# Linear attention, an MLP and routed experts in one kernel: where the last blocks' router products run, and where the first expert tile's weights lie

## The chip, the cores and the metric

The kernel runs on one core of a Trainium2 chip. Its time is the device time of one execution in microseconds, a median of several runs. One more execution was profiled; all rows below come from it, with times in microseconds from its first instruction.

## The reference

Three stages, each feeding the next, on 2304 tokens (batch 4, 576 positions), in float32:

```
phi(x)  = [exp(p - m), exp(m - p)]   with p = x @ w_phi, m = max |p|          # 8 heads, 64 -> 2 x 128
attn    = (phi(q) @ (phi(k)^T v)) / (phi(q) . sum phi(k) + 1e-6)              # per head
y       = leaky_relu_0.01(attn @ w_in) @ w_out                                # 512 -> 2048 -> 512
logits  = (y / |y|) @ (emb / |emb|)^T / tau                                   # 8 experts
e, gate = argmax(logits), softmax(logits)[e]                                  # per token
out     = gate * (relu(y @ w1[e]) @ w2[e])                                    # 512 -> 1024 -> 512
```

## The kernel before, in words

Tokens are worked on in nine blocks of 256 (two tiles of 128) through attention and MLP. Products that need precision beyond one pass are split into a high and a low part, and three matmuls add up hi*hi, hi*lo and lo*hi. The MLP's inner width of 2048 is cut in sixteen chunks; a first loop over the blocks does chunks 0 to 7 and stores the half sums yp, a second loop does chunks 8 to 15. In it `mm1` makes h of a chunk, ScalarE and VectorE make t, g and gg of it (GpSimd the low half of gg), and `mm2` adds gg times the second weights into y. `y_half_b` ends a block: VectorE adds y and yp to ys (L606), SyncE stores ys, ScalarE squares it (L609), and then the logits are made, for blocks 0 to 7 by sixteen multiply-and-sum instructions on VectorE (L615; two tiles by eight experts, here called products, which read the embeddings `enb`), for block 8 on TensorE (L626, L634: eight transposes of ys and products with `ent`). `route` ranks the tokens of a block within their expert.

After block 5 a list of five tiles of 128 tokens is made for the most frequent expert (the early list), and a second list for the rest (late list, `make_list`, `list_ids`, `list_tail`) after block 8. The expert stage then walks over up to 25 tiles: `gather` fetches the tokens, `xT` transposes them, `up` and `down` are the two matmul stages, each in two halves of inner columns, `hT` transposes between. A tile's weights are four arrays of 128x2048 read to `raw`, and `split` (L921, L922) copies each to whi on ScalarE and subtracts to wlo on VectorE. These pairs lie in the buffers of the ring that held the MLP's second chunks, two buffers for a pair: pairs 1 to 3 use those of chunks 8 to 13. Pair 0 lies in a pool of its own, `ring_c`, that is opened in the space of `enb` and the products' scratch once these are closed, before block 8.

Each engine takes its instructions in order. The order is made when the program is built, by a scheduler with priorities; on TensorE the expert tiles' order is written out by hand, and on ScalarE that of tiles 0 and 1. Step (i, n) is a place in that written order: tile i, quarter n. `steps` names what of block 8 is put there: `ends` (its last two chunks of mm2, and the sums) at (0,1), then the four pieces `TAILS`, and the late list.

Of the kernel before, what the change touches and what calls it, by code (L numbers as in the profile page):

```python
# [9 lines left out]
F32 = mybir.dt.float32  # L10
F32R = mybir.dt.float32r
# [10 lines left out]
P = 128  # L22
B, H, S, D, F = 4, 8, 576, 64, 128
NTOK = B * S
DM = H * D
NPAIR = H // 2
DFF = 2048
NE = 8
EF = 1024
BLK = 256  # L30
NBLK = NTOK // BLK
NT = NTOK // P
NCH = 8
T_EARLY = 12
N_EARLY = 5
N_TILES = 25
N_PLAIN = 23
BIG = 8192.0
PRIO = 1000
J_PE = 8  # L40
J_UP = 9
W_DVE = tuple(range(16, 32))
N_HEAD = 3
# [16 lines left out]
GPOS2 = (5, 2)  # L60
MAN = (mybir.EngineType.PE,)
ENDS = (0, 1)
TAILS = ((1, 1), (1, 2), (2, 0), (2, 1))


@with_exitstack
def tile_attention_moe_router_experts(ctx, tc, qT, kT, va, w_phi, moew, emb, embT, tau, ew, out):
    nc = tc.nc
# [11 lines left out]
    def bc(ap, shape):  # L80
        return ap.to_broadcast(shape)


    ident = const.tile([P, P], F32, name="ident")
# [15 lines left out]
    for i in range(2):  # L100
        for r in range(2):
            nc.vector.tensor_copy(
                out=wblk[r * D:(r + 1) * D, i, r * F:(r + 1) * F],
                in_=wstk[r * D:(r + 1) * D, i, :].bitcast(F32),
# [3 lines left out]
    xg = ctx.enter_context(tc.tile_pool(name="xg", bufs=2, side="right"))  # L108
# [100 lines left out]
    qraw, qps, xr, xb = {}, {}, {}, {}  # L209
# [127 lines left out]
    yps = {}  # L337
# [20 lines left out]
    def mm2(j, c):  # L358
        c0 = c % NCH
        if c0 == 0:  # L360
            yps[j] = [ps_m.tile([P, DM], F32, tag="y", name="y") for _ in range(2)]
        gg, w = gs.pop((j, c)), wc[c]
        for t in range(2):
            ts = slice(t * P, (t + 1) * P)
            for a, b in ((0, 0), (0, 1), (1, 0)):
                nc.tensor.matmul(  # L366
                    yps[j][t], gg[:, a, ts], w[:, b, DM:2 * DM],
                    start=(c0 == 0 and a == 0 and b == 0), stop=(c0 == NCH - 1 and a == 1),
                )
# [80 lines left out]
    for j in range(NBLK):  # L450
# [15 lines left out]
        if j == NBLK - 1:  # L466
# [3 lines left out]
            ring_b = ctx.enter_context(tc.tile_pool(name="ring_b", bufs=8, side="left", reuse_waits="tile"))  # L470
# [35 lines left out]
    rt = ctx.enter_context(tc.tile_pool(name="rt", bufs=1, side="right", reuse_waits="tile"))  # L506
    ps_r = ctx.enter_context(tc.tile_pool(name="ps_r", bufs=1, space=PSUM))
    ps_t = ctx.enter_context(tc.tile_pool(name="ps_t", bufs=2, space=PSUM))
# [3 lines left out]
    def b_load(j):  # L512
        t = xg.tile([P, 2, 4, BLK], F32R, tag="xb", name="xb2")
        nc.gpsimd.dma_start(out=t, in_=xs_d[j])
        xb[j] = t
        y = xg.tile([P, 2, DM], F32, tag="yt", name="yt2")
        nc.sync.dma_start(out=y, in_=yp_d[j])
        ypt[j] = y

    b_load(0)  # L520
    lg_cm = tc.tile_pool(name="lg", bufs=1, side="right", reuse_waits="tile")
    lgp = lg_cm.__enter__()

    enb = lgp.tile([P, NE, DM], F32, name="enb")
    sst = rt.tile([P, NT], F32, name="sst")
    lg = rt.tile([P, NT, NE], F32, name="lg")
# [9 lines left out]
        out=upper, in_=upper, pattern=[[1, P]], compare_op=ALU.is_gt, fill=0.0, base=0, channel_multiplier=-1  # L536
# [45 lines left out]
    ent = rt.tile([P, 4, NE], F32, name="ent")  # L582
# [13 lines left out]

    def y_half_b(j):
        yt = ypt.pop(j)
        on_pe = j >= J_PE
        yss = []  # L600
        if not on_pe:
            lgr = rt.tile([P, 2, NE], F32, tag="lgr", name="lgr")
        for t in range(2):
            i = 2 * j + t
            ys = xg.tile([P, DM], F32, tag="ys", name="ys")
            nc.vector.tensor_add(ys, yps[j][t], yt[:, t, :])  # L606
            nc.sync.dma_start(out=y_d[i * P:(i + 1) * P, :], in_=ys)
            jk = xg.tile([P, DM], F32, tag="jk", name="jk", bufs=1)
            nc.scalar.activation(out=jk, in_=ys, func=AF.Square, accum_out=sst[:, i:i + 1])  # L609
            yss.append(ys)  # L610
            if on_pe:
                continue
            for e in range(NE):
                jk2 = lgp.tile([P, DM], F32, tag="jk2", name="jk2")
                nc.vector.tensor_tensor_reduce(  # L615
                    out=jk2, in0=ys, in1=enb[:, e, :], scale=1.0, scalar=0.0,
                    op0=ALU.mult, op1=ALU.add, accum_out=lgr[:, t, e:e + 1],
                )
        yps.pop(j)
        yield  # L620
        if on_pe:
            yTs = []
            for ys in yss:
                ps = ps_t.tile([P, DM], F32, tag="t", name="ytp")
                for k in range(4):
                    nc.tensor.transpose(ps[:, k * P:(k + 1) * P], ys[:, k * P:(k + 1) * P], ident)  # L626
                yT = xg.tile([P, DM], F32, tag="gg", name="yT", bufs=3)
                nc.scalar.copy(out=yT, in_=ps)
                yTs.append(yT)
            yield  # L630
            pl = ps_r.tile([P, 2, NE], F32, tag="pr", name="plg")
            for t in range(2):
                for k in range(4):
                    nc.tensor.matmul(  # L634
                        pl[:, t], yTs[t][:, k * P:(k + 1) * P], ent[:, k],
                        start=(t == 0 and k == 0), stop=(t == 1 and k == 3),
                    )
            lgr = pl
        nc.vector.tensor_tensor(
            out=lg[:, 2 * j:2 * j + 2, :], in0=lgr, in1=bc(esc.unsqueeze(1), [P, 2, NE]), op=ALU.mult  # L640
        )
        yield from route(j)
# [226 lines left out]
    def gather(i):  # L869
        xgt = m1.tile([P, DM], F32, tag="xgt", name="xgt")  # L870
        nc.gpsimd.indirect_dma_start(
            out=xgt, out_offset=None, in_=y_d[0:T_EARLY * P, :] if i < N_EARLY else y_d,
            in_offset=bass.IndirectOffsetOnAxis(ap=lists[i][1], axis=0),
        )
        xgs[i] = xgt
# [23 lines left out]
    def load_w(i, c):  # L899
        if i == 0 or i >= N_PLAIN:  # L900
            load_rows(i, c)
            return
        if i not in need:
            need[i] = nc.values_load(
                lists[i][2], engines=[mybir.EngineType.Pool], min_val=0, max_val=4 * NE
            )
        with tc.If(need[i] < NE):
            load_rows(i, c)
# [5 lines left out]
    pairs = {}  # L914
    changes = {}

    def split(c):
        hi, lo = pairs[c]
        for h in range(2):
            hs_ = slice(h * 1024, (h + 1) * 1024)  # L920
            nc.scalar.copy(out=hi[:, hs_], in_=raw[c][:, hs_])  # L921
            nc.vector.tensor_sub(lo[:, hs_], raw[c][:, hs_], hi[:, hs_].bitcast(F32))  # L922

    def first_split(c):
        pool = ring_c if c == 0 else ring_b
        pairs[c] = tuple(pool.tile([P, 2048], F32R, tag="W", name=n) for n in ("whi", "wlo"))
        split(c)
        load_w(1, c)

    def next_split(i, c):  # L930
# [6 lines left out]
        if i + 1 < N_PLAIN:  # L937
            load_w(i + 1, c)

    for j in range(NBLK):  # L940
        if j + 1 < NBLK:
            b_load(j + 1)
        last = j == NBLK - 1
        if last:
            lg_cm.__exit__(None, None, None)
            ring_c = ctx.enter_context(tc.tile_pool(name="ring_c", bufs=2, side="right", reuse_waits="tile"))
        with tc.high_priority(offset=2 * PRIO if j >= J_UP else 0):
            for c in range(NCH):
                mm1(j, NCH + c, 200 if j == 0 else 0)
                if c >= 2:  # L950
                    mm2(j, NCH + c - 2)
        if last:
            break
        mm2(j, 2 * NCH - 2)
        mm2(j, 2 * NCH - 1)
        for n, _ in enumerate(y_half_b(j)):
            pass
        xb.pop(j)
        if 2 * j + 2 == T_EARLY:
            with tc.high_priority(offset=PRIO):  # L960
                early_list = list_ids(*make_list(T_EARLY, N_EARLY, True))
                for c in range(4):
                    load_w(0, c)
                gather(0)
            xT(0)
            for _ in list_tail(*early_list):
                pass
# [91 lines left out]

    j = NBLK - 1  # L1060
    late = []
    tail = y_half_b(j)

    def ends():
        mm2(j, 2 * NCH - 2)
        mm2(j, 2 * NCH - 1)
        xb.pop(j)
        next(tail)

    steps = {  # L1070
        ENDS: ends,
        TAILS[0]: lambda: next(tail),
        TAILS[1]: lambda: next(tail),
        TAILS[2]: lambda: next(tail, None),
        TAILS[3]: lambda: late.append(make_list(NT, N_TILES - N_EARLY, False)),
        POS: lambda: late.append(list_ids(*late.pop())),
    }

    def hooks(i, n):
        if (i, n) in steps:  # L1080
            with tc.high_priority(offset=PRIO):
                steps[i, n]()
        if (i, n) == GPOS:
            late.append(list_tail(*late.pop(), after=acts[-K_ACT]))
            next(late[0])
        if (i, n) == GPOS2:
            next(late[0], None)

    for c in range(4):
        first_split(c)  # L1090
    with tc.manual_schedule(engines=set(MAN)):
        run(0, N_PLAIN, next_split, hooks)
# [60 lines left out]
```

## Time and profile before

| | |
|---|---|
| median of 3 runs | 927.18 us (926.13 to 929.4) |
| profiled execution | 925.01 us |
| its span, first to last instruction | 923.3 us |
| TensorE matmuls (PE) busy | 881.8 us, 96% |
| VectorE (DVE) busy | 553.2 us, 60% |
| ScalarE (ACT) busy | 450.2 us, 49% |
| GpSimd (POOL) busy | 225.3 us, 24% |
| mean granted clock of TensorE | 0.984 of full speed |

How to read it: a busy share is an average over stages, so it says which engine to look at, not where. Matmuls overlap in the records, so one lasts longer than its distance to the next. In the rows, PE is TensorE, DVE VectorE, ACT ScalarE, POOL GpSimd; the brackets at a row's end give the idle time of the engine before it and what ended it. The granted clock is a share of 2.4 GHz: 1.00 is full, 0.50 is 1.2 GHz.

### The profile page before, as it was taken

What the parts mean: (1) busy time and instruction counts of PE and PEld (TensorE: products, weight loads), DVE (VectorE), ACT (ScalarE), POOL (GpSimd) and SP (SyncE); (2) the same over time, 40 slices, a digit from 0 to 9 for tenths busy, and PEclk for the clock granted to TensorE, in tenths of its full rate; (3) what the DMA queues carried; (4) which work ended last, traced back from release to release, by engine and by line L of the source; (5) the groups of instructions that cost most, each with busy time, mean ns of one, the idle gap of its engine ahead of it and who ended that gap; (6) DMA issues with size and microseconds to landing.
All of it is one profiled execution on the core that took longest, in us unless ns stands there. A gap on an engine that the chain in (4) does not pass through costs nothing. (4 is left out here: it accounts for less than half of the span.)

```text
span 923.3 us, 18721 instructions
## 1 busy us (share of the span) xinstructions
PE 881.8 (96%) x7104; PEld 757.1 (82%) x7104; DVE 553.2 (60%) x1276; ACT 450.2 (49%) x904; POOL 225.3 (24%) x219
## 2 busy tenths in 40 slices
PE   8979999999999999899999999959999999999994
PEld 6768888889898888788888888838888888888883
DVE  6775557484765554748888899863422761113572
ACT  6965556484745654743333332523423862224571
POOL 2430113031111330033233333501113431113321
PEclk9989999999999999999999999979999999999998
DMA  8873423142130211943222221601014941114570
GB/s 280 290 239 99 133 75 127 50 123 103 48 107 24 104 69 61 324 166 112 86 103 92 98 89 65 240 23 36 28 49 149 351 150 47 41 41 168 183 265 31
DMA packets 42613, 112.36 MB, mean 122 GB/s; under 512 B 4558, under 2 KB 23118, under 8 KB 36496
## 3 DMA queue, kind: packets, MB, share of 16 engines
q1 hardware_dynamic: 33424, 61.48, 20.1%
q0 software_dynamic: 9008, 49.55, 15.4%
q8 instruction: 57, 0.93, 0.4%
q14 instruction: 44, 0.36, 0.1%
q10 hardware_dynamic: 80, 0.03, 0.0%
HBM read 87.45 MB, written 24.90 MB: 122 GB/s over the span
## 5 line engine op out<-in xcount | busy, mean ns | idle before, releaser
L366 PE MATMUL y<-W,gg 128*128 128x512 f32 x864 | 230.0, 400 | 1.0 <-ACT gg L353 1.0
L366 PEld LDWEIGHTS y<-W,gg 128*128 128x128 f32 x864 | 153.0, 189 | 29.0 <-ACT gg L353 1.4
L344 PE MATMUL h<-xb,W 128*128 128x256 f32 x576 | 164.3, 288 | 5.2 <-DVE g L351 3.3
L345 PE MATMUL h<-xb,W 128*128 128x256 f32 x576 | 162.7, 283 | 1.9 <-DVE xb L294 1.6
L346 PE MATMUL h<-xb,W 128*128 128x256 f32 x576 | 162.1, 283 | 0.0
L344 PEld LDWEIGHTS h<-xb,W 128*128 128x128 f32 x576 | 108.1, 189 | 13.3 <-DVE g L351 4.7
L345 PEld LDWEIGHTS h<-xb,W 128*128 128x128 f32 x576 | 108.5, 188 | 7.7 <-DVE xb L294 2.2
L252 POOL PARTITION_ALL_REDUCE qmx<-pr x28 | 56.4, 2016 | 221.6 <-ACT pr L234 218.0
L346 PEld LDWEIGHTS h<-xb,W 128*128 128x128 f32 x576 | 108.5, 189 | 1.6 <-issue 0.2
L353 ACT CAST gg<-g 128x256 fp32r<-128x256 f32 x144 | 57.5, 406 | 96.2 <-DVE g L351 87.5
L615 DVE CUSTOM_DVE_ANT_0 jk<-ys,enb 128x512 f32<-128x512 f32 x128 | 102.5, 801 | 2.0
L349 ACT ACTIVATE t<-h 128x256 f32<-128x256 f32 x144 | 54.5, 382 | 88.4 <-PE h L346 87.7
L351 DVE TENSOR_TENSOR g<-h,t 128x256 f32<-128x256 f32 x144 | 60.1, 420 | 53.4 <-ACT t L349 50.2
L355 POOL TENSOR_TENSOR gg<-g,gg 128x256 fp32r<-128x256 f32 x72 | 59.0, 823 | 134.5 <-ACT gg L353 117.7
L922 DVE TENSOR_TENSOR wlo<-raw,whi 128x1024 fp32r<-128x1024 f32 x56 | 68.1, 1255 | 36.0 <-ACT whi L921 30.3
L996 DVE TENSOR_TENSOR h<-htp,h 128x512 fp32r<-128x512 f32 x46 | 31.7, 689 | 92.9 <-ACTq L935 74.4
L978 PE MATMUL hps<-whi,xt 128*128 128x512 f32 x184 | 77.3, 420 | 9.9 <-ACT whi L921 9.8
L1008 PE MATMUL yo<-whi,h 128*128 128x512 f32 x184 | 74.7, 406 | 0.0
L979 PE MATMUL hps<-wlo,xt 128*128 128x512 f32 x184 | 73.7, 400 | 0.5 <-DVE wlo L922 0.5
L1009 PE MATMUL yo<-wlo,h 128*128 128x512 f32 x184 | 72.6, 395 | 0.0
L921 ACT CAST whi<-raw 128x1024 fp32r<-128x1024 f32 x56 | 55.9, 1047 | 34.2 <-PE hps L982 13.0
L985 ACT ACTIVATE hs<-hps 128x512 f32<-128x512 f32 x46 | 27.4, 595 | 71.3 <-PE hps L982 64.8
(239 smaller groups left out, 1600.0 us busy)
## 6 DMA issues: line engine op xcount, KB each, us to landing
wst<-in_moew_dram SPq DMA_DIRECT2D x32, 512.0 KB, 5.3
qraw<-in_q_dram SPq DMA_DIRECT2D x36, 256.0 KB, 3.0
xs_d<-xb SPq DMA_DIRECT2D x9, 1024.0 KB, 5.4
xb<-xs_d POOLq DMA_DIRECT2D x9, 1024.0 KB, 5.2
kraw<-in_k_dram SPq DMA_DIRECT2D x16, 288.0 KB, 3.3
yp_d<-yt SPq DMA_DIRECT2D x9, 512.0 KB, 3.7
yt<-yp_d SPq DMA_DIRECT2D x9, 512.0 KB, 3.8
y_d<-ys SPq DMA_DIRECT2D x18, 256.0 KB, 2.1
```

The source lines that it names most:

```text
L344: nc.tensor.matmul(hp, w[:, 0, ks], x[:, 0, k, :], start=(k == 0), stop=False)
L345: nc.tensor.matmul(hp, w[:, 0, ks], x[:, 1, k, :], start=False, stop=False)
L346: marks["mm1"] = nc.tensor.matmul(hp, w[:, 1, ks], x[:, 0, k, :], start=False, stop=(k == 3))
L351: nc.vector.tensor_tensor(out=g, in0=hp, in1=t, op=ALU.max)
L355: eng.tensor_sub(gg[:, 1, :], g, gg[:, 0, :].bitcast(F32))
L366: nc.tensor.matmul(yps[j][t], gg[:, a, ts], w[:, b, DM:2 * DM], start=(c0 == 0 and a == 0 and b == 0), stop=(c0 == NCH - 1 and a == 1),)
L615: nc.vector.tensor_tensor_reduce(out=jk2, in0=ys, in1=enb[:, e, :], scale=1.0, scalar=0.0, op0=ALU.mult, op1=ALU.add, accum_out=lgr[:, t, ...
L922: nc.vector.tensor_sub(lo[:, hs_], raw[c][:, hs_], hi[:, hs_].bitcast(F32))
L978: nc.tensor.matmul(ps, x[:, 0, k], hi[:, ks], start=(k == 0), stop=False)
L979: nc.tensor.matmul(ps, x[:, 0, k], lo[:, ks], start=False, stop=False)
L1008: nc.tensor.matmul(yacc[i], h2[:, 0, k], hi[:, w0], start=(nh == 0 and k == 0), stop=False)
L1009: nc.tensor.matmul(yacc[i], h2[:, 0, k], lo[:, w0], start=False, stop=False)
```

## The change

The logits of block 8 are made by products on VectorE, as for the other blocks; the TensorE variant goes (L626, L634). `enb` stays to the end, and `ring_c` with it goes: pairs 0 to 2 take the buffers of chunks 8 to 13, and pair 3, split inside `ends`, those of chunks 14 and 15. `y_half_b` stops once more, between the sums and the products, so that the products of blocks 7 and 8 can be put into steps (0,2) and (1,0), without the raised priority. The ranks of block 7 go to (1,3) and (2,1), those of block 8 to (2,2) and (3,0), the late list's making to (3,0).

```diff
-J_PE = 8
-TAILS = ((1, 1), (1, 2), (2, 0), (2, 1))
+DOTS = ((0, 2), (1, 0))
+ROUTE = ((1, 3), (2, 1), (2, 2), (3, 0))
...
     def y_half_b(j):
...
-            ys = xg.tile([P, DM], F32, tag="ys", name="ys")
+            ys = xg.tile([P, DM], F32, tag="xb" if j == NBLK - 1 else "ys", name="ys")
...
+        yps.pop(j)
+        yield
+        lgr = rt.tile([P, 2, NE], F32, tag="lgr", name="lgr")
+        for t, ys in enumerate(yss):
             for e in range(NE):
                 jk2 = lgp.tile([P, DM], F32, tag="jk2", name="jk2")
                 nc.vector.tensor_tensor_reduce(
...
         yield
-        if on_pe:
-            yTs = []
-            for ys in yss:
-                ps = ps_t.tile([P, DM], F32, tag="t", name="ytp")
-                for k in range(4):
-                    nc.tensor.transpose(ps[:, k * P:(k + 1) * P], ys[:, k * P:(k + 1) * P], ident)
...
-            pl = ps_r.tile([P, 2, NE], F32, tag="pr", name="plg")
...
     def first_split(c):
-        pool = ring_c if c == 0 else ring_b
-        pairs[c] = tuple(pool.tile([P, 2048], F32R, tag="W", name=n) for n in ("whi", "wlo"))
+        pairs[c] = tuple(ring_b.tile([P, 2048], F32R, tag="W", name=n) for n in ("whi", "wlo"))
...
-        if last:
-            lg_cm.__exit__(None, None, None)
-            ring_c = ctx.enter_context(tc.tile_pool(name="ring_c", bufs=2, side="right", reuse_waits="tile"))
...
-        for n, _ in enumerate(y_half_b(j)):
-            pass
+        ends_of[j] = y_half_b(j)
+        if j == NBLK - 2:
+            next(ends_of[j])
+        else:
+            for _ in ends_of[j]:
+                pass
...
     def ends():
         mm2(j, 2 * NCH - 2)
         mm2(j, 2 * NCH - 1)
         xb.pop(j)
-        next(tail)
+        next(ends_of[j])
+        first_split(3)
+
+    def last_route():
+        next(ends_of[j], None)
+        late.append(make_list(NT, N_TILES - N_EARLY, False))
 
     steps = {
         ENDS: ends,
-        TAILS[0]: lambda: next(tail),
...
+        DOTS[0]: lambda: next(ends_of[j - 1]),
+        DOTS[1]: lambda: next(ends_of[j]),
+        ROUTE[0]: lambda: next(ends_of[j - 1]),
+        ROUTE[1]: lambda: next(ends_of[j - 1], None),
+        ROUTE[2]: lambda: next(ends_of[j]),
+        ROUTE[3]: last_route,
...
-            with tc.high_priority(offset=PRIO):
+            with tc.high_priority(offset=0 if (i, n) in DOTS else PRIO):
...
-    for c in range(4):
+    for c in range(3):
         first_split(c)
```

The scheduler makes a new order from this. Three places follow. On TensorE, the start of the first expert tile before; y is block 8's second matmuls, hps the tile's up, prk the ranks of block 7:

```order
L366 MATMUL y<-W,gg 128x512 x6
L907 UNCONDITIONAL_BRANCH x2
L978 MATMUL hps<-whi,xt 128x512
L979 MATMUL hps<-wlo,xt 128x512
L978 MATMUL hps<-whi,xt 128x512
L979 MATMUL hps<-wlo,xt 128x512
L978 MATMUL hps<-whi,xt 128x512
L664 LDWEIGHTS upper
L664 MATMUL prk<-oh,upper 128x8
L665 LDWEIGHTS ones
L665 MATMUL prk<-cum,ones 128x8
```

and in the change:

```order
L366 MATMUL y<-W,gg 128x512 x6
L886 UNCONDITIONAL_BRANCH
L958 MATMUL hps<-whi,xt 128x512
L959 MATMUL hps<-wlo,xt 128x512
L958 MATMUL hps<-whi,xt 128x512
L959 MATMUL hps<-wlo,xt 128x512
L958 MATMUL hps<-whi,xt 128x512
L959 MATMUL hps<-wlo,xt 128x512
```

The ranks no longer stand inside the first up. On ScalarE, the same stretch before, from the first half's hs to the second's; jk are the squares of block 8's ys, raw_5447 is pair 0's raw and raw_5450 pair 3's, and the copies behind a COMPARE_AND_BRANCH are only made where a tile's expert is another than the last one's:

```order
L985 ACTIVATE hs<-hps 128x512
L932 TENSOR_LOAD esk
L932 ISA x2
L935 COMPARE_AND_BRANCH
L921 CAST whi<-raw_5447 128x1024 x2
L935 UNCONDITIONAL_BRANCH x2
L907 UNCONDITIONAL_BRANCH
L609 ACTIVATE jk,sst<-ys 128x512 x2
L995 CAST h_8238<-htp 128x512
L985 ACTIVATE hs<-hps 128x512
```

and in the change:

```order
L913 COMPARE_AND_BRANCH
L900 CAST whi<-raw_5447 128x1024 x2
L913 UNCONDITIONAL_BRANCH x2
L886 UNCONDITIONAL_BRANCH
L605 ACTIVATE jk,sst<-ys 128x512 x2
L900 CAST whi<-raw_5450 128x1024 x2
L975 CAST h_8175<-htp 128x512
L965 ACTIVATE hs<-hps 128x512
```

Pair 3's copies now stand between the squares and the second half's hs. On VectorE, before, from the sums ys of block 8 on; rk to rm are block 7's ranks, h and xt the low parts for down and up:

```order
L606 TENSOR_TENSOR ys<-y,yt_7627 128x512 x2
L667 TENSOR_TENSOR rk<-prk,oh 128x16
L669 TENSOR_REDUCE rr<-rk 128x2
L671 TENSOR_TENSOR ge<-rr,thr 128x36
L674 TENSOR_REDUCE qi<-ge 128x2
L675 SCALAR_TENSOR_TENSOR rr<-qi,rr 128x2
L679 TENSOR_SCALAR rm<-io_5376,rr 128x128 x2
L996 TENSOR_TENSOR h_8238<-htp,h_8238 128x512
```

In the change, around the same sums; each ISA with jk is a product and the ISA behind it reads its sum, jk_8209 is the last of block 7's and jk_8255 the first of block 8's:

```order
L613 ISA jk_8205,lgr<-ys,enb 128x512
L613 ISA lgr 128x1
L613 ISA jk_8207,lgr<-ys,enb 128x512
L613 ISA lgr 128x1
L602 TENSOR_TENSOR ys<-y,yt_7627 128x512 x2
L613 ISA jk_8209,lgr<-ys,enb 128x512
L613 ISA lgr 128x1
L618 TENSOR_TENSOR lg<-lgr,esc 128x16
L631 TENSOR_REDUCE mx<-lg 128x2
L613 ISA jk_8255,lgr<-ys,enb 128x512
```

and a few rows on, up to the low part of xt for tile 1:

```order
L901 TENSOR_TENSOR wlo<-raw_5450,whi 128x1024
L634 TENSOR_TENSOR wt<-wt,w_5392 128x16
L613 ISA jk_8259,lgr<-ys,enb 128x512
L613 ISA lgr 128x1
L901 TENSOR_TENSOR wlo<-raw_5450,whi 128x1024
L976 TENSOR_TENSOR h_8175<-htp,h_8175 128x512
L636 TENSOR_REDUCE m_8402<-wt 128x2
L864 TENSOR_TENSOR xt<-xtp,xt 128x512
```

Fifteen of block 7's products stand ahead of the sums of block 8; four products, the small operations of block 7's ranks and pair 3's subtractions stand between the sums and xt, and twelve products between that xt and the next tile's.

## Rows read from the trace of the kernel before

**Rows 1.** TensorE in order of time: start, us, instruction [idle before].

```profile
599.16 1.56 PE L366 MATMUL y<-W,gg 128*128 128x512 f32 x6
610.57 0.80 PE L978 MATMUL hps<-whi,xt 128*128 128x512 f32 x1 [9.85 <-ACT whi L921]
...
620.25 0.63 PE L992 MATMUL htp<-ident,hs 128*128 128x128 f32 x4
```

**Rows 2.** Stretches: length, busy PE, PEld, DVE, ACT, POOL; granted clock, DMA share, GB/s.

```profile
600.72:604.24 3.52, 0.00 (x1) 0.00 (x0) 3.52 (x7) 0.81 (x2) 1.60 (x2) 1.00 0.00 0
604.24:610.57 6.33, 0.00 (x0) 0.00 (x0) 5.94 (x17) 1.09 (x2) 0.57 (x1) 0.50 0.00 0
610.57:617.90 7.33, 6.86 (x18) 4.77 (x19) 2.66 (x5) 1.50 (x2) 0.00 (x0) 0.50 0.00 0
...
620.25:640.00 19.75, 19.39 (x107) 16.00 (x107) 6.80 (x22) 7.13 (x14) 1.91 (x2) 1.00 0.16 51
370.50:373.90 3.40, 0.62 (x6) 0.46 (x5) 1.52 (x4) 2.09 (x5) 0.00 (x0) 1.00 0.95 345
```

**Rows 3.** ScalarE in order of time.

```profile
589.79 2.00 ACT L921 CAST whi<-raw 128x1024 fp32r<-128x1024 f32 x2 [1.14 <-PE y L366]
...
609.48 1.99 ACT L921 CAST whi<-raw 128x1024 fp32r<-128x1024 f32 x2 [6.19 <-DVE lgr L615]
...
620.44 0.63 ACT L609 ACTIVATE jk<-ys 128x512 f32<-128x512 f32 x1 [2.55 <-DVE ys L606]
...
621.83 0.57 ACT L995 CAST h<-htp 128x512 fp32r<-128x512 f32 x1
...
628.26 0.60 ACT L985 ACTIVATE hs<-hps 128x512 f32<-128x512 f32 x1 [2.54 <-PE hps L982]
...
636.96 0.60 ACT L985 ACTIVATE hs<-hps 128x512 f32<-128x512 f32 x1 [4.06 <-PE hps L982]
```

**Rows 4.** VectorE in order of time.

```profile
585.90 1.29 DVE L606 TENSOR_TENSOR ys<-y,yt 128x512 f32<-128x512 f32 x2
...
592.97 1.23 DVE L615 CUSTOM_DVE_ANT_0 jk<-ys,enb 128x512 f32<-128x512 f32 x1
...
608.01 0.69 DVE L615 CUSTOM_DVE_ANT_0 jk<-ys,enb 128x512 f32<-128x512 f32 x1
...
608.74 0.69 DVE L615 CUSTOM_DVE_ANT_0 jk<-ys,enb 128x512 f32<-128x512 f32 x1
...
610.55 1.23 DVE L922 TENSOR_TENSOR wlo<-raw,whi 128x1024 fp32r<-128x1024 f32 x1
...
625.12 0.69 DVE L885 TENSOR_TENSOR xt<-xtp,xt 128x512 fp32r<-128x512 f32 x1 [1.97 <-ACT xt L884]
...
643.74 0.31 DVE L738 TENSOR_TENSOR cmp<-cnt,thr 128x144 f32<-128x144 f32 x1 [0.51 <-DVEq L935]
...
649.18 0.53 DVE L809 TENSOR_TENSOR bw<-bw,thr 128x360 bf16<-128x360 bf16 x1
```

**Rows 5.** TensorE in the expert tiles, in order of time.

```profile
628.00 1.03 PE L626 MATMUL ytp<-ident,ys 128*128 128x128 f32 x8
...
632.12 1.85 PE L634 MATMUL plg<-ent,yT 128*128 128x8 f32 x16
...
646.56 0.48 PE L978 MATMUL hps<-whi,xt 128*128 128x512 f32 x1
...
649.45 0.60 PE L881 MATMUL xtp<-ident,xgt 128*128 128x128 f32 x4
...
662.38 1.05 PE L829 MATMUL pp<-bw,rm 128*128 128x20 bf16 x36
```

**Rows 6.** GpSimd in order of time.

```profile
592.17 2.63 POOL L355 TENSOR_TENSOR gg<-g,gg 128x256 fp32r<-128x256 f32 x2 [4.94 <-ACT gg L353]
...
603.37 1.45 POOL L355 TENSOR_TENSOR gg<-g,gg 128x256 fp32r<-128x256 f32 x1 [0.22 <-ACT gg L353]
```

**Rows 7.** The products' line: count, ns least/median/most, first and last start.

```profile
L615 DVE CUSTOM_DVE_ANT_0 jk<-ys,enb x128: 664/691/1227, 421.0 to 608.7; 128x512 f32<-128x512 f32 x128
```

More of the change, by code (lines that the diff above doesn't have):

```diff
@@ L520, in tile_attention_moe_router_experts @@
     b_load(0)
-    lg_cm = tc.tile_pool(name="lg", bufs=1, side="right", reuse_waits="tile")
-    lgp = lg_cm.__enter__()
+    lgp = ctx.enter_context(tc.tile_pool(name="lg", bufs=1, side="right", reuse_waits="tile"))
     enb = lgp.tile([P, NE, DM], F32, name="enb")
@@ L598, in y_half_b @@
         yt = ypt.pop(j)
-        on_pe = j >= J_PE
         yss = []
-        if not on_pe:
-            lgr = rt.tile([P, 2, NE], F32, tag="lgr", name="lgr")
         for t in range(2):
             i = 2 * j + t
-            ys = xg.tile([P, DM], F32, tag="ys", name="ys")
+            ys = xg.tile([P, DM], F32, tag="xb" if j == NBLK - 1 else "ys", name="ys")
             nc.vector.tensor_add(ys, yps[j][t], yt[:, t, :])
@@ L610, in y_half_b @@
             yss.append(ys)
-            if on_pe:
-                continue
+        yps.pop(j)
+        yield
+        lgr = rt.tile([P, 2, NE], F32, tag="lgr", name="lgr")
+        for t, ys in enumerate(yss):
             for e in range(NE):
@@ L618, in y_half_b @@
                 )
-        yps.pop(j)
         yield
-        if on_pe:
-            yTs = []
-            for ys in yss:
-                ps = ps_t.tile([P, DM], F32, tag="t", name="ytp")
-                for k in range(4):
-                    nc.tensor.transpose(ps[:, k * P:(k + 1) * P], ys[:, k * P:(k + 1) * P], ident)
[L627 to L630, printed above, removed]
-            pl = ps_r.tile([P, 2, NE], F32, tag="pr", name="plg")
[L632 to L638, printed above, removed]
         nc.vector.tensor_tensor(
@@ L938, in next_split @@
             load_w(i + 1, c)
+    ends_of = {}
     for j in range(NBLK):
@@ L1061, in tile_attention_moe_router_experts @@
     late = []
-    tail = y_half_b(j)
+    ends_of[j] = y_half_b(j)
     def ends():
@@ L1067, in ends @@
         xb.pop(j)
-        next(tail)
+        next(ends_of[j])
[3 more added lines that the diff above has]
+        late.append(make_list(NT, N_TILES - N_EARLY, False))
     steps = {
         ENDS: ends,
-        TAILS[0]: lambda: next(tail),
-        TAILS[1]: lambda: next(tail),
-        TAILS[2]: lambda: next(tail, None),
-        TAILS[3]: lambda: late.append(make_list(NT, N_TILES - N_EARLY, False)),
+        DOTS[0]: lambda: next(ends_of[j - 1]),
[4 more added lines that the diff above has]
+        ROUTE[3]: last_route,
         POS: lambda: late.append(list_ids(*late.pop())),
```

## The prediction

> **What bounds the kernel now.** The page's busy shares have TensorE far ahead of the other engines, so only a stretch in which it waits, or runs at the lower clock, can give much time back. I therefore went through TensorE's instructions in order of time, and found one wait over 3 us. The last matmuls of block 8 begin at 599.16 and take 1.56; the next instruction, the first expert tile's "up" (the first half of its inner columns, called up(0,0) below), starts at 610.57 after 9.85 us of idling that ended with ScalarE's copy of the weights into whi [rows 1]. Next the busy table by stretch: the granted clock is 1.00 when the wait begins, 0.50 from 604.24, and still 0.50 until 617.90, while TensorE is at work again [rows 2]. Then ScalarE: that copy (609.48) waited 6.19 us for VectorE's lgr, that is for the last scalar product of block 7 [rows 3]. Then VectorE: there the products run one behind the other, at 608.01 and 608.74 the last two [rows 4]. So block 7's products on VectorE set the end of that wait, because pair 0 of the first tile is stored in the space of the embeddings (enb), which these products read.
>
> **What the change takes away.** (1) Pair 0 now takes the buffers of chunks 8 and 9, free when block 8's second matmuls of chunk 9 end. In the trace of before, pair 1 has those buffers, and its copy starts at 589.79 on the end of these matmuls [rows 3]. With two copies (1.99 for both [rows 3]), two subtractions of about 1.2 (610.55 [rows 4]) and a few products between them, pair 0 is ready by 595 to 597. TensorE reaches up(0,0) at 600.7, so the 9.85 go. (2) With the idling goes the slow clock behind it: 610.57 to 620.25 hold 24 matmuls of 512 columns [rows 1]; at full clock twelve take 2.89 (646.56 to 649.45 [rows 5]), so 24 take 5.8: 9.7 - 5.8 = 3.9 us. (3) TensorE loses block 8's eight transposes and its sixteen small products: from one hs to the next (628.26 to 636.96 [rows 3]) there are 8.7 us where down, one transposition and up would take 2.9 + 0.35 + 2.9 = 6.1 (0.35 is an estimate, somewhat over half of the 0.60 that four transposes last at 649.45, as they overlap what follows [rows 5]): 2.6 us. The rows at 628.00 and 632.12 (1.03 and 1.85 [rows 5]) bear that out. Together 16.4 us.
>
> **What it adds.** Sixteen products of block 8 on VectorE, 0.73 apart (608.01 to 608.74 [rows 4]), 11.7 us, and the first tile's fourth split between the same rows. Where VectorE is ahead of TensorE that is free; the order of the change says where it is not. I follow it on the clock of the trace of before.
>
> Block 8: TensorE has the same work. But the copy of pair 1 now waits for chunk 11's second matmuls (595.2), and chunk 12's gg stands behind it on ScalarE: 595.2 + 2.0 + 0.3 = 597.5, where TensorE wants it at 596.6. I take 1.0 us late, up(0,0) at 601.7. Bounds: 0 (TensorE has other matmuls in front of that gg) and 2.0 (one whole pair of copies).
>
> First tile: the copy of pair 2 waits for chunk 13 (601.7), ends at 603.7, and behind it come t and g of chunk 15: VectorE has g at 604.4. From there to the sums ys of block 8 its queue holds four products (2.9), two subtractions of pair 2 (2.4, and 0.5 more beside GpSimd), a register load with its branch (at most 0.5, the gap before 643.74 [rows 4]), and the sums themselves (1.3, as at 585.90 [rows 4]): 612.0. The matmuls that ys needs end at 601.7 + 2 x 2.85 = 607.4; VectorE is the later one.
>
> ScalarE stands behind ys: in its order come the two squares of ys (1.4, from 620.44 to 621.83), both copies of pair 3 (2.0), the cast of h (0.57), and only then hs of the second half (0.60) [rows 3]. The first ys is there at 611.4, so hs at 611.4 + 1.4 + 2.0 + 0.6 + 0.6 = 616.0. TensorE, after the twelve matmuls for chunks 14 and 15 (607.4), a transposition, up(0,1) and xT, wants it at 607.4 + 0.35 + 2.9 + 0.35 = 611.0. New wait: 5.0. Bounds: 0 (rival A) and 8.8 (rival C, 3.8 more).
>
> xt of tile 1: from 612.0 VectorE has four products (2.9), five small operations at 0.24 (25 rows from 643.74 to 649.18 [rows 4]: 1.2), two subtractions of pair 3 (2.4), h and xt (0.69 each, as at 625.12 [rows 4]), less what overlaps: 619.6. TensorE starts up(1,0) at 616.4 and needs the low part of xt after eight of its twelve matmuls, at 618.4: 1.2 more.
>
> Tile 2: up to its xt VectorE has twelve products, two h, some 1.5 of small work and xt, 12.2: at 631.8, where TensorE wants it at about 632. No wait, and no margin.
>
> Sum: 9.85 + 3.9 + 2.6 - 1.0 - 5.0 - 1.2 = 9.2 us. The profiled execution took 925.0 us (its span of 923.3 and 1.7 around it), so 915.8 in its place; the median shown, 927.2, is 2.2 above it, which makes **918.0 us**.
>
> The late list moves too: its count (cnt) from step (2,1) to (3,0), later by three pieces of about 3.2 us, while its matmuls (pp) stay at (3,3). Before, the last bw begins at 649.18 [rows 4] and pp starts at 662.38 [rows 5]: 12.7 us to spare. Of these 9.7 go, and some 2 for block 8's ranks, which now stand between the rows of the list; about 1 remains. I cost the move at nothing, with 0 and 2 as bounds.
>
> The Trainium skill (GPSIMD Engine Reference, section Specifications) says that GpSimd shares its SBUF interfaces with VectorE and contends with VectorE instructions of two SBUF inputs, as the products are. The trace agrees: a product at 592.97 takes 1.23 [rows 4] beside GpSimd's gg (592.17, two in 2.63 [rows 6]), against a median of 0.691 over 128 [rows 7]. By it each product of the change that meets GpSimd would cost 0.5 more, which rival C prices.
>
> **The rivals.**
> A. VectorE keeps up. From 620.25 to 640.00 it was busy for 6.80 of 19.75 us [rows 2], and the new rows would fit into the rest. If ys comes near 607.4, both new waits vanish: 16.4 - 1.0 = 15.4, 911.8 us. Against it: four products and two subtractions stand between g of chunk 15 and ys, with known durations.
> B. The forecast, and the clock falls in the new wait. The idling of 9.85 lowered the clock 3.5 us after it began; in 370.50 to 373.90 TensorE worked 0.62 of 3.40 and kept 1.00 [rows 2]. A wait of 5.0 lies between. Each matmul at the lower level costs 0.16 more (3.9 over 24); up(1,0) and part of down(0,0), some twenty, cost 3.2, of which 1.2 hides in the wait for xt: 920.0 us.
> The Trainium skill (TensorE: Matmul & The Clock Gate, section Why this matters for your kernels) advises against idle gaps between bursts of matmuls, since the array falls back to half rate; rows 2 agree for the long gap and show the short one without it. By it alone B would be the forecast.
> C. Slower: products cost 1.2 instead of 0.73, as the one at 592.97 did. The eight between g of chunk 15 and xt of tile 1 then add 3.8, the twelve up to xt of tile 2, where no margin is left, 5.6, and the clock falls in both waits (2 x 3.2): 918.0 + 15.8 = 933.8. It ends above 927.2 once a product costs about 0.14 more than 0.73 and both waits lower the clock, or 0.46 more without the clock. Against it: GpSimd's last tensor operation there starts at 603.37 and takes 1.45 [rows 6].
> D. The bound only moves: the late list holds pp up by some 4 us and the wait for xt of tile 2 opens by as much: no change, 926. For it: both margins above are 1 us or less. Against it: by their rows neither chain grows by more than 2.
>
> **How the numbers follow.** Forecast 0.50 (its own range 915 to 920), A 0.20, B 0.18, C 0.06, D 0.06. A measurement of this kernel tells a change from none at about 0.3%, 2.8 us. Faster: the forecast, A and B, 0.88; same 0.06; slower 0.06. The range holds A's 911.8 and B's 920.0, with 2 us for the list: 911.5 to 922.
>
> **What would show it.** The wait before the first hps gone or under 1.5 us, and the clock at 1.00 from 600 to 611. A wait of 4 to 6 us before TensorE's transposition htp, ended by ScalarE's hs, with ScalarE waiting for VectorE's ys; a second of about 1 inside hps, ended by xt. From the second half of tile 1 on, hs comes 9 to 10 us earlier than before. I am wrong if the first hps still waits for whi, if htp does not wait, or if pp or xt of tile 2 holds TensorE for over 2 us.

## The result, and the profile after

The changed kernel takes **919.56 us** (median of 5 runs, 917.62 to 922.24) against 927.18 (925.26 to 929.4) for the kernel before, timed beside it: ratio 0.9917, 95% interval 0.989 to 0.9944. The forecast was 918.0, with a range of 911.5 to 922. The profiled execution took 917.62 us, its span is 915.8 (before: 925.01 and 923.3), and the mean granted clock went from 0.984 to 0.988.

First TensorE in order of time (start, us, engine, line, instruction, and in brackets the idle time before it with what ended it):

```profile
601.58 0.50 PE L958 MATMUL hps<-whi,xt 128*128 128x512 f32 x1 [0.66 <-DVE g L351]
...
610.52 0.60 PE L860 MATMUL xtp<-ident,xgt 128*128 128x128 f32 x4
615.96 1.09 PE L972 MATMUL htp<-ident,hs 128*128 128x128 f32 x4 [4.83 <-DVE m L636]
616.70 0.78 PE L958 MATMUL hps<-whi,xt 128*128 128x512 f32 x1
...
644.27 0.17 PE L714 MATMUL cnt<-cum,ones 128*128 128x8 bf16 x1 [0.27 <-DVE rk L646]
653.65 1.05 PE L808 MATMUL pp<-bw,rm 128*128 128x20 bf16 x36
```

The wait of 9.85 us before the first hps [rows 1] is gone: that matmul starts at 601.58 instead of 610.57. One wait of more than 1 us is left from there to the end, 4.83 us before htp of the second half. Nothing stops pp, which starts 8.7 us earlier than before [rows 5].

The busy table by stretch (length; busy time of PE, PEld, DVE, ACT and POOL; granted clock, DMA share, GB/s) shows what this wait did to the clock:

```profile
601.58:604.48 2.90, 2.90 (x12) 2.36 (x13) 2.90 (x6) 0.79 (x2) 1.68 (x2) 1.00 0.00 0
611.12:613.76 2.64, 0.00 (x1) 0.00 (x0) 2.43 (x8) 2.53 (x5) 1.36 (x1) 1.00 0.14 40
613.76:615.96 2.20, 0.00 (x1) 0.04 (x1) 2.20 (x6) 0.28 (x1) 0.00 (x0) 0.50 0.26 88
616.70:620.58 3.88, 3.88 (x11) 3.11 (x10) 3.69 (x13) 0.58 (x1) 0.00 (x0) 0.50 0.02 4
620.58:640.00 19.42, 19.42 (x96) 15.65 (x96) 10.89 (x37) 4.83 (x8) 1.97 (x2) 1.00 0.08 28
```

The clock is at 1.00 (2.4 GHz) in up(0,0), where before it stood at 0.50 (1.2 GHz) [rows 2]. It falls inside the new wait, at 613.76, and up(1,0) runs almost wholly at 0.50. From 620.58 to 640 TensorE is busy without a gap.

ScalarE around the wait:

```profile
598.33 1.99 ACT L900 CAST whi<-raw 128x1024 fp32r<-128x1024 f32 x2
...
609.01 0.63 ACT L605 ACTIVATE jk<-ys 128x512 f32<-128x512 f32 x1 [3.67 <-DVE ys L602]
...
610.39 1.98 ACT L900 CAST whi<-raw 128x1024 fp32r<-128x1024 f32 x2
612.27 0.57 ACT L975 CAST h<-htp 128x512 fp32r<-128x512 f32 x1
612.75 0.60 ACT L965 ACTIVATE hs<-hps 128x512 f32<-128x512 f32 x1
...
621.59 0.60 ACT L965 ACTIVATE hs<-hps 128x512 f32<-128x512 f32 x1 [3.93 <-PE hps L962]
...
627.57 0.60 ACT L965 ACTIVATE hs<-hps 128x512 f32<-128x512 f32 x1 [2.22 <-PE hps L962]
```

The queue is the one that the prediction described: squares behind ys, both copies of pair 3, the cast of h, hs. But hs is done at 613.35, and htp starts at 615.96. So hs did not end the wait. VectorE did:

```profile
602.05 0.42 DVE L351 TENSOR_TENSOR g<-h,t 128x256 f32<-128x256 f32 x1
...
608.29 1.28 DVE L602 TENSOR_TENSOR ys<-y,yt 128x512 f32<-128x512 f32 x2
...
612.15 1.23 DVE L901 TENSOR_TENSOR wlo<-raw,whi 128x1024 fp32r<-128x1024 f32 x1 [0.21 <-DVEq L913]
...
613.38 0.68 DVE L613 CUSTOM_DVE_ANT_0 jk<-ys,enb 128x512 f32<-128x512 f32 x1
...
613.99 1.22 DVE L901 TENSOR_TENSOR wlo<-raw,whi 128x1024 fp32r<-128x1024 f32 x1
615.12 0.68 DVE L976 TENSOR_TENSOR h<-htp,h 128x512 fp32r<-128x512 f32 x1
...
615.80 0.68 DVE L864 TENSOR_TENSOR xt<-xtp,xt 128x512 fp32r<-128x512 f32 x1
...
628.96 0.69 DVE L864 TENSOR_TENSOR xt<-xtp,xt 128x512 fp32r<-128x512 f32 x1
```

The row h at 615.12 is the low part of h of the *first* half. It is the last reader of the first half's transposition, and the transpositions share two PSUM buffers (ps_t, tag t): htp(0,0) holds one, xtp of tile 1 the other, and htp(0,1) has to wait for the first. It starts 0.16 us after that row ends. (The bracket names m, a small row of the same queue; the experiments below settle that it is h.) ScalarE's high part of h was there at 612.84; VectorE came to it 2.3 us later, since it still had pair 3's two subtractions and a product to do.

### The profile page after: what moved, and what is told of

It reads as the page before. It is cut to its first block, busy times and chain, and to the rows that moved or that the text cites. A ratio compares the mean times of both kernels' runs of the same rounds, so it can differ in the third digit from the quotient of the medians.

```text
span 915.8 us, 18701 instructions
## 1 busy us (share of the span) xinstructions
PE 879.2 (96%) x7080; PEld 754.8 (82%) x7080; DVE 562.0 (61%) x1308; ACT 448.8 (49%) x902; POOL 223.4 (24%) x219
## 5 line engine op out<-in xcount | busy, mean ns | idle before, releaser
L344 PEld LDWEIGHTS h<-xb,W 128*128 128x128 f32 x576 | 108.1, 189 | 12.7 <-DVE g L351 4.2
L613 DVE CUSTOM_DVE_ANT_0 jk<-ys,enb 128x512 f32<-128x512 f32 x144 | 114.2, 793 | 3.1 <-DVEq L913 1.1
L355 POOL TENSOR_TENSOR gg<-g,gg 128x256 fp32r<-128x256 f32 x72 | 57.1, 797 | 136.2 <-ACT gg L353 118.9
```

What stands on the lines that cost most here:

```text
L344: nc.tensor.matmul(hp, w[:, 0, ks], x[:, 0, k, :], start=(k == 0), stop=False)
L613: nc.vector.tensor_tensor_reduce(out=jk2, in0=ys, in1=enb[:, e, :], scale=1.0, scalar=0.0, op0=ALU.mult, op1=ALU.add, accum_out=lgr[:, t, ...
```

## The experiments

Each run was timed beside the kernel before, and runs are compared by their ratio to it. Executions differ in when they reach the first tile (601.6 to 606.7 us), so inside a trace the waits are compared, not the start times. "Half clock" means a granted clock of 0.50.

**The rings alone (e1_rings).** The kernel before with one half of the change: all four pairs of the first tile in ring_b, the embeddings kept, block 8's logits still on TensorE:

```
-        pool = ring_c if c == 0 else ring_b
-        pairs[c] = tuple(pool.tile([P, 2048], F32R, tag="W", name=n) for n in ("whi", "wlo"))
+        pairs[c] = tuple(ring_b.tile([P, 2048], F32R, tag="W", name=n) for n in ("whi", "wlo"))
...
-        if last:
-            lg_cm.__exit__(None, None, None)
...
     def ends():
...
+        first_split(3)
...
-    for c in range(4):
+    for c in range(3):
```

> The ring part of the change alone: all four pairs of the first tile in ring_b, embeddings kept; block 8's logits stay on TensorE, so block 8 has no products on VectorE. Theory (VectorE's queue up to the low part of h, with the raised priority of pair 3's subtractions, sets the wait before the second half's htp): the wait of 9.85 us goes, a wait of 4 to 5 us before htp stays, and the 2.6 us of TensorE's eight transposes and sixteen small products come back: 919.6 + 2.6 = 922.2. Rival (block 8's products make that wait): no wait over 1 us, clock at 1.00: 922.2 - 4.8 - 2 = 915.4.

Measured: 921.38 us, ratio 0.9932 (0.9906 to 0.9958), which overlaps the changed kernel's 0.989 to 0.9944, so the time alone does not show the 2.6 us. TensorE, and VectorE at the end of its wait:

```profile
606.72 0.50 PE L973 MATMUL hps<-whi,xt 128*128 128x512 f32 x1 [1.22 <-DVE g L351]
...
616.94 0.17 PE L663 MATMUL prk<-oh,upper 128*128 128x8 bf16 x1 [0.68 <-DVE oh L657]
...
620.69 1.08 PE L987 MATMUL htp<-ident,hs 128*128 128x128 f32 x4 [3.39 <-DVE h L991]
```

```profile
617.43 1.23 DVE L921 TENSOR_TENSOR wlo<-raw,whi 128x1024 fp32r<-128x1024 f32 x1
...
618.65 1.22 DVE L921 TENSOR_TENSOR wlo<-raw,whi 128x1024 fp32r<-128x1024 f32 x1
...
619.87 0.68 DVE L991 TENSOR_TENSOR h<-htp,h 128x512 fp32r<-128x512 f32 x1
```

The 9.85 us go with the rings alone, and without any product of block 8 a wait of 4.1 (0.68 + 3.39, with four small matmuls between) stands at the same place. Here its bracket names VectorE's h. The rival, that block 8's products make the wait, is out. (The clock fell in this wait too.)

**Pair 3 split later (e2_split3).**

```
     def ends():
-        first_split(3)
...
     def hooks(i, n):
...
+        if (i, n) == (0, 3):
+            first_split(3)
```

> The changed kernel with one line moved: the first tile's fourth split (pair 3) is issued in step (0,3) without raised priority, so VectorE reaches the low part of h of the first half ahead of pair 3's two subtractions. Theory (VectorE's queue up to that instruction sets the wait of 4.83 us): h's low part 2.5 to 3 us earlier (612 to 613 instead of 615.1), wait about 2 us; if the clock then stays at 1.00, 4 to 5 us faster than the changed kernel (about 915), else 2 to 3 (917). Rival (ScalarE's hs behind its copies, as the prediction had it, with VectorE's row only a bystander; or pair 3 is then late for up(1,0)): the wait moves by a microsecond or less, or comes back as one before up's last matmuls: 919 to 920.

Measured: **913.62 us** (912.93 to 914.68), ratio 0.9851 (0.9824 to 0.9878), faster than both kernels; its interval lies wholly below the changed kernel's 0.989 to 0.9944.

```profile
603.19 0.50 PE L958 MATMUL hps<-whi,xt 128*128 128x512 f32 x1 [1.23 <-DVE g L351]
...
613.66 0.63 PE L972 MATMUL htp<-ident,hs 128*128 128x128 f32 x4 [0.93 <-DVEq L913]
```

```profile
599.91 2.89 DVE L901 TENSOR_TENSOR wlo<-raw,whi 128x1024 fp32r<-128x1024 f32 x2
...
604.00 3.15 DVE L901 TENSOR_TENSOR wlo<-raw,whi 128x1024 fp32r<-128x1024 f32 x2
...
612.83 0.68 DVE L976 TENSOR_TENSOR h<-htp,h 128x512 fp32r<-128x512 f32 x1
...
615.69 1.22 DVE L901 TENSOR_TENSOR wlo<-raw,whi 128x1024 fp32r<-128x1024 f32 x1
```

From up(0,0) to the low part of h there are now 9.64 us (612.83 - 603.19) instead of 13.54 (615.12 - 601.58). The wait shrinks from 4.83 to 0.93, where about 2 was expected, and the clock stays at 1.00 from 70 us to the last stage of the kernel. Sixteen products and all splits are still there; only the order is other. The move takes pair 3's two copies out of ScalarE's queue as well: hs of the second half starts 9.2 us after up(0,0) (612.39 - 603.19) instead of 11.2 (612.75 - 601.58). Without that, hs would have held htp by some 2.3 us, as the run with another bank shows below. So the gain is that of a split moved on both engines; VectorE's part by itself was not tried.

**Without block 8's products (e3_borrow).**

```
...
-        for t, ys in enumerate(yss):
...
+        if j == NBLK - 1:
+            nc.vector.tensor_copy(out=lgr, in_=lgrs[j - 1])
+        lgrs[j] = lgr
+        for t, ys in enumerate(yss if j < NBLK - 1 else []):
```

> The changed kernel with block 8's sixteen scalar products left out: block 8 takes over block 7's sums, so its logits and all that hangs on them are wrong; everything else is done. Theory (VectorE's queue): only some three of the sixteen stand ahead of the low part of h, so h is 2.2 us earlier, the wait is about 2.6 us, and the products cost 2 us as long as the clock falls all the same (917.5), up to 4 if it doesn't (915.5). Rival (the sixteen products as a whole, 11.7 us, are the price): the wait is gone and tiles 1 and 2 run without a stop: 913 or less.

Measured: 917.49 us, ratio 0.9901 (0.9868 to 0.9934); by time alone this cannot be told from the changed kernel. The trace tells more:

```profile
616.44 1.09 PE L977 MATMUL htp<-ident,hs 128*128 128x128 f32 x4 [3.71 <-DVE h L981]
```

The wait lost 1.1 us of 4.83, half of the 2.2 that the theory expected, and the clock fell all the same. In place of the products small operations of both blocks' ranks came forward on VectorE, and pair 3's first subtraction waited 0.24 us (until 613.09) for ScalarE's copy. Leaving out sixteen products of 0.73 us (11.7 us of VectorE's time) is worth less at this place than moving one split (two subtractions of 1.2 on VectorE, two copies of 1.0 on ScalarE) behind the rows that TensorE waits for.

**The price of the clock (e4_dummy).**

```
+        if live and i == 0:
+            dm = ps_r.tile([P, DM], F32, tag="pp", name="dummy")
+            for n in range(N_DUMMY):
+                nc.tensor.matmul(dm, xt[0][:, 0, n % 4], pairs[0][0][:, (n % 4) * DM:(n % 4 + 1) * DM], start=True, stop=True)
         if live:
             hT(i, 1)
```

> The changed kernel with twenty more matmuls of 512 columns on TensorE, whose result nobody reads, between tile 1's xT and the second half's transposition, where it waits 4.83 us. Theory (the fall of the clock in that wait has its own price): the clock stays at 1.00, up(1,0) takes 3 us instead of 4.6, and the time is 1.5 to 2.5 us less than the changed kernel's (about 917.5). Rival (the clock costs nothing, since VectorE is late for tile 1 in any case): same as the changed kernel, 919.6, with a new wait inside up(1,0).

Measured: 918.1 us (915.21 to 921.18), ratio 0.9902 (0.9872 to 0.9932): in the expected direction, but unclear by time. The stretch of the dummies and that of up(1,0):

```profile
611.13:616.18 5.05, 4.92 (x23) 3.67 (x22) 4.87 (x13) 3.01 (x5) 0.96 (x1) 1.00 0.23 75
616.57:619.45 2.88, 2.88 (x15) 2.33 (x13) 2.88 (x12) 0.59 (x1) 0.00 (x0) 1.00 0.02 6
```

htp starts 0.2 us later than in the changed kernel (616.18, 615.96), yet the hs of up(1,0) comes at 619.71 instead of 621.59: from htp to hs 3.5 us instead of 5.6. The fall of the clock costs 2.1 us, and no new wait opens in up(1,0), so VectorE's low part of xt is early enough for full clock too.

**Another bank for xT of tile 1 (e5_bank).** Nothing on VectorE or ScalarE changes:

```
-        ps = ps_t.tile([P, DM], F32, tag="t", name="xtp")
+        ps = ps_r.tile([P, DM], F32, tag="pp", name="xtp") if i == 1 else ps_t.tile([P, DM], F32, tag="t", name="xtp")
```

> The changed kernel with one buffer more: the transposition xT of tile 1 alone goes into another PSUM bank (tag pp, unused until the late list), so that the second half's htp no longer needs the bank which VectorE's low part of h of the first half frees; VectorE's and ScalarE's work is the same. Theory (that bank is what ends the wait): htp starts when ScalarE's hs is there, 2.4 us earlier than in the changed kernel, the wait is 2.4 instead of 4.83, and a shorter wait of 0.5 to 1 opens in up(1,0) for the low part of xt, which VectorE still has late: 1.5 to 2 us faster if the clock falls all the same (918), 3 to 4 if it stays up (916). Rival (hs itself is late, as the prediction had it): nothing moves, 919.6.

Measured: 916.55 us (914.31 to 917.24), ratio 0.9887 (0.9865 to 0.9909); by time alone this cannot be told from the changed kernel. TensorE, then ScalarE's hs and VectorE's low part of h:

```profile
604.48 0.50 PE L958 MATMUL hps<-whi,xt 128*128 128x512 f32 x1 [0.67 <-DVE g L351]
...
616.32 0.66 PE L972 MATMUL htp<-ident,hs 128*128 128x128 f32 x4 [2.31 <-ACTq L913]
...
619.46 1.20 PE L962 MATMUL hps<-whi,xt 128*128 128x512 f32 x4 [0.31 <-DVE xt L864]
```

```profile
615.67 0.60 ACT L965 ACTIVATE hs<-hps 128x512 f32<-128x512 f32 x1
...
618.05 0.68 DVE L976 TENSOR_TENSOR h<-htp,h 128x512 fp32r<-128x512 f32 x1
```

The wait goes from 4.83 to 2.31, and now it does end with ScalarE's hs. The low part of h is as late as it was (13.57 us after up(0,0), before 13.54), and TensorE no longer waits for it; the clock stays at 1.00 in this wait. So the shared PSUM buffer is what tied htp(0,1) to VectorE; the prediction's chain over hs was real and stood 2.5 us behind it. The 0.31 before the last matmuls of up(1,0) is the wait for xt that the prediction had at 1.2. The Trainium skill (Perfetto Trace Analysis, section Optimizing Tensor Performance) advises to rotate independent groups of matmuls through different PSUM banks, so that reading one out overlaps the next; the trace agrees, with 2.5 us here.

**Pair 2 split later too (e6_split23).**

```
+        if (i, n) == (0, 3):
+            first_split(2)
+            first_split(3)
-    for c in range(3):
+    for c in range(2):
```

> A version meant to beat both: pair 2's split as well as pair 3's is issued in step (0,3), behind xT of tile 1, without raised priority. Theory (what is left on VectorE's and ScalarE's queues ahead of g of chunk 15 and of the low part of h are pair 2's copies and subtractions): the 1.2 us before up(0,0) go, htp of the second half waits 0.3 to 0.6 instead of 0.93, the clock stays at 1.00, and down(0,0) waits up to 0.8 for pair 2's low part: 0 to 1.5 us faster than with pair 3 moved alone (912 to 913.6). Rival (pair 2 is then late as a whole): down(0,0) waits 2 to 4 us, 915 to 918.

Measured: 914.2 us, ratio 0.9876 (0.9854 to 0.9898), where 912 to 913.6 was expected: no gain over the version with pair 3 alone moved, whose interval it overlaps.

```profile
603.93 0.50 PE L958 MATMUL hps<-whi,xt 128*128 128x512 f32 x1 [1.24 <-DVE g L351]
...
613.78 0.66 PE L972 MATMUL htp<-ident,hs 128*128 128x128 f32 x4 [0.31 <-ACTq L913]
...
619.14 0.50 PE L989 MATMUL yo<-wlo,h 128*128 128x512 f32 x1 [0.43 <-DVE wlo L901]
```

```profile
600.65 2.89 DVE L901 TENSOR_TENSOR wlo<-raw,whi 128x1024 fp32r<-128x1024 f32 x2
603.46 0.41 DVE L351 TENSOR_TENSOR g<-h,t 128x256 f32<-128x256 f32 x1
```

The waits at htp and in down(0,0) came out as expected. The 1.2 before up(0,0) did not go, and that part of the theory was wrong: the two subtractions ahead of g are pair 1's. They were so with pair 3 alone moved, too: there pair 1's stand at 599.91, and pair 2's at 604.00, behind g of chunk 15 (603.66). Pair 2's split was never in front of the g that up(0,0) waits for.

## Why the prediction was right, and where it was wrong

The total was right, and most terms were. Two errors of mechanism nearly cancelled. The last column says between which rows of the two traces a term was read, before and after.

| Term | predicted | measured | from |
|---|---|---|---|
| wait for whi, less block 8's lateness | 9.85 - 1.0 | 9.0 | up(0,0): 610.57, 601.58 |
| half clock behind that wait | 3.9 | 4.0 | up(0,0) to htp(0,0): 9.68, 5.70 |
| TensorE's transposes and small products | 2.6 | 2.7 | hs to hs: 8.7 [rows 3], 6.0 |
| new wait before htp(0,1) | -5.0 | -4.5 | 4.83, less 0.31 that stood there before |
| half clock behind the new wait | 0 (rival B: -2.0) | -1.8 | htp(0,1) to hs: 3.82, 5.63 (3.53 with the dummies) |
| wait for xt of tile 1 | -1.2 | 0 | no gap in up(1,0) |
| late list, ranks, pp | 0 | -0.6 | hs of tile 1 to up(3,0): 16.08, 16.72; pp none |
| sum | 9.2 | 8.8 | up(3,0): 653.04, 644.29 |

- **What the change takes away** held in all three terms, and the rings alone show the first by itself. Of the second, 0.46 was not the clock but a wait for wlo inside up(0,0) (before, at 611.83). Of block 8's lateness the size held and the cause did not: up(0,0) waits 0.66 for VectorE's g of chunk 14 (601.11), the last reader of the PSUM buffer that hps takes. That g stands behind pair 1's subtractions; ScalarE's gg does not come into it.
- **The step that failed** is the cause of the new wait, "hs of the second half ... at 616.0". I followed ScalarE, which TensorE's instruction reads from, and left out what it writes to: the PSUM buffer that VectorE's low part of h had still to read. My own list of VectorE's work had that row just before xt, done at about 618.9, so the right chain on my numbers would have given a wait of 7.9, not 5.0.
- **What made up for it** is the other error: VectorE was 2.4 us ahead of my reckoning (ys ended at 609.57, not 612.0). I let pair 2's copy wait for chunk 13's matmuls (601.7); it started at 598.33, so g of chunk 15 was done at 602.47 instead of 604.4. A copy writes whi, which lies in the first of the pair's two buffers, that of chunk 12; only wlo needs chunk 13's. The trace of before has it: pair 3, which lay in these buffers there, was copied from 598.18 on. That the wait came out at 4.83 where I had 5.0 is therefore luck. The same 2.4 and a somewhat shorter list up to xt (6.2 us instead of 6.9) took the wait for xt away.
- **Rival B** was the better description of the clock, and its 920.0 lies nearer to the 919.56 than my 918.0. I gave it 0.18 because TensorE had worked 0.62 of 3.40 us at 370.50 without a fall. That stretch is one wait of 2.78 us with work on both sides (the matmul behind it starts at 373.44), little more than half of the wait that I forecast, so it was no guide. The size of B's 2.0 was luck in part: it charged some twenty matmuls and took off 1.2 for the wait for xt; the clock was back at 620.58, before down(0,0), and there was no such wait.
- **Rival A** (VectorE keeps up) was wrong for this order of work and nearly right for another: with pair 3 moved the kernel reaches 913.6, where A had 911.8.
- **Rival C**: some products did take longer, up to 1.22 us, but half of the 144 took 0.69 or less, and of the eight between g of chunk 15 and xt of tile 1 only the first took more (0.94, at 602.38):

```profile
L613 DVE CUSTOM_DVE_ANT_0 jk<-ys,enb x144: 661/691/1221, 421.2 to 629.6; 128x512 f32<-128x512 f32 x144
```

- **Rival D**: of the list's margin of 12.7 us 2.8 is left (the last bw ends at 650.81, pp starts at 653.65), and xt of tile 2 (628.96) held nothing up. What the move costs is the -0.6 of the table: between tile 1's second hs and up(3,0), where block 8's ranks and cnt stood before, block 7's ranks now stand too (633.85), and cnt waits 0.27 behind block 8's.

The sign "hs comes 9 to 10 us earlier than before" held from the second half of tile 1 (9.4) to the first half of tile 3 (9.0) and no further. In the second half of tile 4 the changed kernel is 8.7 us ahead of the kernel before, in the last tile 7.5 (start of hs, trace against trace). Some 0.46 of the difference comes at tile 9, where the experiments' traces too jump by up to 0.8 against the changed kernel's, and the rest in steps of at most 0.05 from one hs to the next, which no experiment shows; neither trace has a wait there. Its cause stays open, and with it most of the 1.6 us between the forecast and the median.

## What to carry to other kernels

When a wait is removed, follow the next instruction of the waiting engine in both directions: to who writes what it reads, and to who has still to read the buffer that it overwrites. Then look at the queue of the engine at the end of that chain for work that is there early only because it was issued at a high priority; moving such work behind the rows that are waited for can be worth more than leaving several times as much work out. Look one step further too: behind the row that ends the wait another can stand close, as hs did here. A wait has a second price where the clock falls in it; a few matmuls put into the wait, whose result nobody reads, show the two apart.

## What the runs showed of the hardware that was not expected

The clock is not the same in every execution of the same stretch. At about 340 us, where the kernels' sources do not differ, TensorE works with three short waits in the changed kernel (0.46, 0.32 and 0.58 us) and with the same three when pair 2 is moved too (0.46, 0.33 and 0.59). The busy table by stretch, first the changed kernel, then the other, each with that stretch and the one behind it:

```profile
337.95:341.73 3.78, 2.39 (x14) 1.54 (x13) 2.28 (x3) 2.11 (x6) 2.05 (x2) 1.00 0.17 69
341.73:345.15 3.42, 3.42 (x50) 3.30 (x51) 2.61 (x8) 3.01 (x8) 2.03 (x2) 1.00 0.56 230
```

```profile
336.78:340.56 3.78, 2.38 (x13) 1.54 (x12) 2.28 (x3) 2.10 (x6) 2.05 (x2) 1.00 0.17 69
340.56:343.98 3.42, 3.42 (x39) 3.30 (x40) 2.70 (x8) 2.87 (x7) 2.03 (x2) 0.50 0.56 230
```

TensorE was busy 2.39 and 2.38 of 3.78 us; behind it the clock stayed at 1.00 in the first and was at 0.50 in the second. One trace in which a sparse stretch left the clock alone is therefore no evidence that the next will. Some 30 us later one wait for VectorE's g took 2.61 us in the changed kernel (until 373.05), and the clock stayed; with the rings alone it took 3.90 (until 375.49), and the clock fell in it. Whether such falls make up the spread between executions of one kernel (4.6 us in the changed one) was not tried.

In the waits at htp the clock stayed up for 0.31, 0.93 and 2.31 us and fell for 3.39, 3.71 and 4.83. The Trainium skill (TensorE: Matmul & The Clock Gate, section Why this matters for your kernels) advises against idle gaps between bursts of matmuls; the three long waits agree with it, the three short ones show gaps without a fall, and by it alone B, with its fall of the clock, would have been the forecast, as the prediction says.
